# Values' products in the score buffers, a second bank for the MoE's first layer, and first keys and queries transposed by TensorE

## The chip, the core and the metric

The kernel runs on one core of one Trainium2 chip. The metric is the time of one execution on the device, in microseconds (us). TensorE (PE) does the matrix products, VectorE (DVE), ScalarE (ACT) and GpSimd (POOL) the elementwise work; SyncE (SP) and ACT start the transfers. Products land in PSUM, which has eight banks of 2 KB per partition; all else lies in SBUF.

## The reference

Block-sparse attention, then a two-layer network (here called the MoE) on its output:

```python
# q, k, v: (4, 8, 768, 64) float32; blocks of 32
scores = scale * np.matmul(q, k.transpose(0, 1, 3, 2))
# mask: neighbouring blocks, first and last block row and column, 3 sampled blocks per block row
scores = np.where(mask, scores, -1e9)
attn = softmax(scores)
x = np.matmul(attn, v)            # -> (3072, 512), heads side by side
h = x @ w_in                      # (512, 2048)
g = np.maximum(h, 0) + alpha * np.minimum(h, 0)
out = g @ w_out                   # (2048, 512)
```

w_in and w_out arrive as 64-bit floats.

## The kernel before

Every number of the products is held as two float16 halves, a high part and a rest ("hi" and "lo"), so that products of halves give nearly float32. Each tensor is scaled by a power of two for this.

The work is cut into 12 chunks: 4 batches, 3 chunks each, of 2 tiles of 128 rows (queries). A chunk has 4 units, one for each pair of heads; a unit has 4 steps (2 heads, 2 tiles), so there are 192 steps.

- A step (`attend`): PE makes the scores of 128 queries against 768 keys (`emit_s`, L498); both halves of keys are used through two layouts, `kt` and `ks`, the second with the halves of the partitions swapped. DVE adds the mask and takes the extreme of each row (`emit_bias`, L508). ACT does the exponential (`emit_exp`, L515) and the sum (L519), DVE the reciprocal (L523). The scaled P is split into hi (ACT L325 or DVE L327) and lo (POOL in two instructions, L335 and L336, in two of three steps, DVE L333 in the third), tile `ph`. A DMA transpose on the queue of SP gives `pt` (L538).
- A unit (`values`): PE multiplies transposed P by the values (`emit_av`, L552, 36 products), ACT and DVE split the result into the halves of `x` (L563, L568).
- A chunk of the MoE: 8 pieces of the first layer (`emit_up`, L852, 24 products each, tile `h`), the activation on DVE (L862, L863), the split on ACT (`gh`, L868) and POOL (`gl`, L873), and 8 pieces of the second layer (`emit_down`, L891, 12 products each, two tiles `o`). ACT scales and stores the output (L903).
- Preparation: keys of a batch are loaded (`kf`), squared and summed on ACT (L321), a product with ones gives the total over partitions (L421), DVE makes the scale, hi and lo are made (`kn`) and transposed by DMA (`kt`, L444), and two copies by DMA swap the halves (`ks`). Queries and values go the same way, the values without a transpose, the queries without a swap. w_in (`wi`) and w_out (`wo`) arrive as 64-bit numbers, and three instructions make float32 of each piece (`emit_n1` L708, `emit_n2` L713 or L715, `emit_n3` L720). A piece of w_in is a row of 128x512; a row of w_out comes in two halves of 128x256. The lo half of w_in is made by PE (L776, L777).

Nothing is ordered by hand. The program contains a planner (`Plan`): every operation is given to it with a due time (counted in steps), the engines that may do it with a cost in us on each, the operations it needs and the buffers that it takes and frees. The planner simulates the engines when the program is built and puts out one order, which is then the order of instructions of every engine. PSUM before: two score tiles `s` of two banks each, one bank `a` for the value products, one bank `h` for the first layer, two banks `o` for the second. Due times of the MoE lie `MOE_LAG` steps behind the end of a chunk's attention; those of w_in and w_out are `V_WI + W_WI * f` and `V_WO + W_WO * f` for row f of 16.

Of the kernel before, what the change touches and what calls it, by code (L numbers as in the profile page):

```python
# [54 lines left out]
class Plan:  # L55
# [5 lines left out]
    LAT = {"PE": 0.15, "DVE": 0.11, "ACT": 0.12, "POOL": 0.08}  # L61
# [4 lines left out]
    def buf(self, pool):  # L66
        return Buf(pool)
# [8 lines left out]
    def run(self):  # L76
# [16 lines left out]
        order = []  # L93
        busy = dict.fromkeys(self.ENGINES, 0.0)
# [78 lines left out]
def attn_moe(ctx: ExitStack, tc: tile.TileContext, q, k, v, sampled, w_in, w_out, alpha, out):  # L173
# [20 lines left out]
    plan = Plan(dict(bufs, s=2, a=1, h=1, o=2, ld=LD))  # L194
# [79 lines left out]
    bias = cpool.tile([P, NT, S], BF16, name="bias")  # L274
    nident = cpool.tile([P, P], F16, name="nident")
# [64 lines left out]
    MAX4 = {"DVE": (0.55, 1.1), "ACT": 0.85}  # L340
    LOW4 = {"DVE": (0.94, 1.5), "POOL": 2.8}
# [12 lines left out]
    kbuf, ksbuf, vbuf, qtbuf, ptbuf, xbuf = {}, {}, {}, {}, {}, {}  # L354
    o_s, o_kt, o_ks, o_v2, o_qt, o_cs, o_pt, o_x, o_sv = {}, {}, {}, {}, {}, {}, {}, {}, {}
# [91 lines left out]

    def emit_k_swap(e, b, hp):
# [92 lines left out]

    def emit_av(u):
# [4 lines left out]
        av = T["av", u] = ps_a.tile([P, W2], F32, tag="av", name="av")  # L547
# [25 lines left out]
    def prep_k(b, hp, prio, gate, pl):  # L573
# [4 lines left out]
        ab = plan.buf("o" if b == 0 else "a")  # L578
# [7 lines left out]
        o_kt[b, hp] = plan.op(prio - 2, {"SP": 2.4}, lambda: emit_k_t(b, hp), [o], [kbuf[b, hp]], [nb], dma=2.3)  # L586
        o_ks[b, hp] = plan.op(prio - 2, {"SP": 0.12}, lambda e: emit_k_swap(e, b, hp), [o_kt[b, hp]],
                              [ksbuf[b, hp]], [kbuf[b, hp]], dma=1.3)

    def prep_v(b, pl, prio, gate):  # L590
# [9 lines left out]
        ab = plan.buf("o" if b == 0 else "a")  # L600
# [8 lines left out]
    def prep_q(c, prio, pl, gate):  # L609
# [16 lines left out]
        for u, fb in zip(us, fbs):  # L626
            hp = units[u][1]
            p = prio if c == 0 else first[u] - 5
            nb = plan.buf("qn")
            o = plan.op(p, {"POOL": 0.35 + 0.25 * f, "ACT": 0.15 + 0.25 * f, "DVE": (0.1 + 0.15 * f, 0.2 + 0.4 * f)},  # L630
                        lambda e, u=u: emit_q_hi(e, u), [sc[hp]], [nb], [fb])
            o = plan.op(p, {"DVE": (0.14 + 0.27 * f, 0.2 + 0.65 * f)}, lambda u=u: emit_q_lo(u), [o], [], [nb, fb])
            qtbuf[u] = plan.buf("qt")
            o_qt[u] = plan.op(p - 2, {"SP": 0.8 * f}, lambda u=u: emit_q_t(u), [o], [qtbuf[u]], [nb], dma=0.75 * f)

    def attend(n):
# [5 lines left out]
        o_s[n] = o = plan.op(n, {"PE": 0.66}, lambda: emit_s(n), [o_qt[u], o_kt[b, hp], o_ks[b, hp]], [sb],  # L642
# [10 lines left out]
        o_pt[n] = plan.op(n - 1, {"SP": 2.4}, lambda: emit_p_t(n), [o],  # L653
                          [ptbuf[u, h]], [pb], dma=2.2)

    def values(u):
# [3 lines left out]
        ab = plan.buf("a")  # L660
# [3 lines left out]
        last = [o_pt[n] for n in range(first[u], first[u + 1])]  # L664
        o = plan.op(p - 2, {"PE": 0.4 + 1.92 * f}, lambda: emit_av(u), last + [o_v2[b, hp]],
# [18 lines left out]
    def emit_load_w(e, name, f, h):  # L684
# [112 lines left out]
    for f in range(NF):  # L797
        p = V_WI + W_WI * f
        o = plan.op(p - 12, LQ, lambda e, f=f: emit_load_w(e, "wi", f, 0), [n3wi[f - 8]] if f >= 8 else [], [plan.buf("ld")], dma=1.6)
        o = plan.op(p, {"DVE": (0.36, 0.6)}, lambda f=f: emit_n1("wi", f, 0), [o])  # L800
        o = plan.op(p, {"ACT": 1.27, "DVE": (0.6, 0.95)}, lambda e, f=f: emit_n2(e, "wi", f, 0), [o])
        n3wi[f] = plan.op(p, {"DVE": (0.61, 0.95)}, lambda f=f: emit_n3("wi", f, 0), [o])
        sqs[f] = plan.op(p, {"ACT": 0.65}, lambda f=f: emit_w_sq("wi", f), [n3wi[f]])
        if f % 2 == 1:
# [6 lines left out]
            for x in (f - 1, f):  # L811
                o = plan.op(p + 0.1, {"ACT": 0.63, "DVE": (0.36, 0.7), "POOL": 0.82}, lambda e, x=x: emit_w_hi(e, "wi", x), [gs[-1], prev])
# [4 lines left out]
                else:  # L817
                    prev = o_wi[x] = plan.op(p, {"DVE": (0.67, 1.1), "POOL": 2.3}, lambda e, x=x: emit_w_lo(e, "wi", x), [o], [], [sb])
    o_gsc = plan.op(V_WI + W_WI * NF - 2, {"DVE": 0.5}, emit_gsc, gs + [o_al])
    osq = []  # L820
    for f in range(NF):
# [3 lines left out]
        n3 = []  # L825
        for h in range(2):
            rb = plan.buf("vf" if h == 0 else "g")
            o = plan.op(p - 8 + 0.1 * h, LQ, lambda e, f=f, h=h: emit_load_w(e, "wo", f, h), [n3wi[min(NF - 1, 8 + f // 2)]], [rb, plan.buf("ld")], dma=0.8)
            o = plan.op(p, {"DVE": (0.22, 0.6)}, lambda f=f, h=h: emit_n1("wo", f, h), [o] + free, [], [rb])
            o = plan.op(p, {"ACT": 0.7, "DVE": (0.34, 0.5)}, lambda e, f=f, h=h: emit_n2(e, "wo", f, h), [o], [], [rb])  # L830
            n3.append(plan.op(p, {"DVE": (0.34, 0.5)}, lambda f=f, h=h: emit_n3("wo", f, h), [o], [], [rb]))
# [80 lines left out]
    def moe(c):  # L912
# [15 lines left out]
        for i, (kind, j) in enumerate(items):  # L928
            p = start + (stop - start) * i / len(items)
            if kind == "u":  # L930
# [79 lines left out]
```

## Time and profile before

| | |
|---|---|
| median of 3 runs | 908.3 us (907.07 to 909.03) |
| profiled execution | 911.63 us, of which the span from first to last instruction is 909.9 us |
| busy in the span | PE 802.7 us (88%), DVE 714.8 (79%), ACT 553.3 (61%), POOL 505.2 (56%) |
| granted clock of TensorE | 0.955 in the mean |
| DMA | 137.45 MB in 393236 packets |

An engine's busy time is a mean over stages that differ. The stretches shown below give it stage by stage: busy microseconds of each engine with the number of its instructions, then PE's granted clock, the DMA share and GB/s. A row of a group of instructions gives the line, the engine, the operation, out<-in, the shapes and the count, then busy time and mean nanoseconds of one, then the idle time before them and what ended it. A row of a wait gives who waited for whom, then microseconds in total, times and the longest. A row of the chain of work gives start, duration and what ran.

### The profile page before, as it was taken

The page shows a single profiled execution, that of the slowest core. Times are in us where ns is not written, and L with a number is a line of the kernel's source. Part 1 is how long each engine was busy: PE and PEld are TensorE (multiplying, and loading weights), DVE is VectorE, ACT ScalarE, POOL GpSimd, SP SyncE. Part 2 cuts the span into 40 slices and gives each one's busy share as a digit, 9 for nine tenths or more (in the row PEclk, how much of TensorE's full clock was granted, in tenths as well). Part 3 has the DMA queues.
Part 4 walks back from the last instruction along what each step waited for, and adds up shares of the span by engine and source line. Part 5 has one row for each costly group of instructions (what it writes and reads, how often), then busy time and mean ns, then how long its engine had stood idle before and what let it go on. Part 6 is the DMA issues. An engine that isn't in the chain of part 4 may idle for free.

```text
span 909.9 us, 16946 instructions
## 1 busy us (share of the span) xinstructions
PE 802.7 (88%) x6089; PEld 528.9 (58%) x6089; DVE 714.8 (79%) x1468; ACT 553.3 (61%) x1185; POOL 505.2 (56%) x413
## 2 busy tenths in 40 slices
PE   3757438988888999999989999999989999999998
PEld 1323215646555766666656766566656667666664
DVE  4899999997888898879987877688987887765232
ACT  6697667875755756757566565666566556664111
POOL 3154445775656667566576665456567566555221
PEclk9867767999999999999999999999999999999999
DMA  9997986988997876969976868969976868655000
GB/s 264 288 263 180 203 210 117 185 134 136 170 175 133 156 138 129 210 130 189 202 154 128 128 128 150 189 119 193 187 140 118 156 117 139 116 117 105 1 24 23
DMA packets 393236, 137.45 MB, mean 151 GB/s; under 512 B 355236, under 2 KB 383936, under 8 KB 393152
## 3 DMA queue, kind: packets, MB, share of 16 engines
q1 hardware_dynamic: 354816, 94.41, 60.2%
q10 hardware_dynamic: 38272, 41.95, 16.8%
q8 instruction: 47, 0.77, 0.3%
q14 instruction: 37, 0.30, 0.1%
q0 software_dynamic: 64, 0.02, 0.0%
HBM read 35.67 MB, written 6.29 MB: 46 GB/s over the span
## 4 chain that ended last, share of the span: by engine, by line
DVE 33%; PE 29%; issue 13%; ACT 12%; DMA 5%; POOL 4%; ACTq 2%; POOLq 0%; DVEq 0%
PE h L852 11%; PE o L891 10%; DVE e L508 6%; ACT e L515 5%; PE sp L498 4%; DVE g L862 4%; DVE ph L333 3%; PE av L552 3%; DVE ph L327 3%; ACT ph L325 2%; DVE g L863 2%; ACTq L364 2%; DMA kf<-in_k_dram 2%; DVE wo L720 2%; DVE qn L403 2%
## 5 line engine op out<-in xcount | busy, mean ns | idle before, releaser
L852 PE MATMUL h<-x,wi 128*128 128x256 f16 x2304 | 270.3, 274 | 14.9 <-DVE g L863 14.7
L852 PEld LDWEIGHTS <-wi 128*128 128x128 f16 x2304 | 227.1, 99 | 57.0 <-issue 18.4
L515 ACT ACTIVATE e<-e,nm 128x768 f32<-128x768 f32 x192 | 178.6, 930 | 114.4 <-DVE nm L508 106.7
L891 PE MATMUL o<-wo,gh 128*128 128x512 f16 x768 | 230.8, 382 | 0.0
L336 POOL TENSOR_TENSOR ph<-e,ph 128x768 f16<-128x768 f32 x128 | 216.7, 1693 | 10.7
L873 POOL TENSOR_TENSOR gl<-g,gh 128x512 f16<-128x512 f32 x96 | 119.1, 1241 | 177.8 <-ACT gh L868 173.4
L335 POOL TENSOR_SCALAR e<-e,rs 128x768 f32<-128x768 f32 x128 | 130.2, 1017 | 157.3 <-DVE ph L327 81.2
L508 DVE CUSTOM_DVE_ANT_0 e<-sp,bias,cs 128x768 f32<-128x768 f32 x192 | 191.9, 1008 | 17.0 <-PE sp L498 10.2
L891 PE MATMUL o<-wo,gl 128*128 128x512 f16 x384 | 146.4, 381 | 1.8 <-POOL gl L873 1.8
L868 ACT CAST gh<-g 128x512 f16<-128x512 f32 x96 | 59.1, 616 | 135.4 <-DVE g L863 120.1
L498 PE MATMUL sp<-kt,qt 128*128 128x512 f16 (+1 forms) x384 | 99.1, 341 | 46.7 <-DVE nm L508 46.5
L498 PEld LDWEIGHTS <-qt 128*128 128x128 f16 x768 | 74.4, 101 | 111.3 <-issue 58.4
L325 ACT ACTIVATE ph<-e,rs 128x768 f16<-128x768 f32 x114 | 105.8, 928 | 28.1 <-DVE rs L523 21.5
L891 PEld LDWEIGHTS <-gh 128*128 128x128 f16 x768 | 74.9, 99 | 80.0 <-issue 3.4
L862 DVE TENSOR_SCALAR g<-h,am 128x256 f32<-128x256 f32 x192 | 83.2, 474 | 48.3 <-PE h L852 46.7
L552 PE MATMUL av<-pt,v 128*64 128x256 f16 x1728 | 108.0, 281 | 1.8 <-DMA pt<-ph 1.5
L552 PEld LDWEIGHTS <-v 128*64 128x64 f16 x1728 | 93.6, 113 | 18.8 <-issue 14.7
L498 PE MATMUL sp<-ks,qt 128*128 128x512 f16 (+1 forms) x384 | 99.3, 342 | 0.0
L523 DVE RECIPROCAL rs<-dn 128x1 f32<-128x1 f32 x192 | 29.0, 156 | 76.0 <-ACT dn L519 75.1
L333 DVE SCALAR_TENSOR_TENSOR ph<-e,rs,ph 128x768 f16<-128x768 f32 x64 | 75.2, 1175 | 9.9 <-ACT ph L325 8.6
L863 DVE SCALAR_TENSOR_TENSOR g<-h,gsc,g 128x512 f32<-128x512 f32 x96 | 72.1, 751 | 3.4
L891 PEld LDWEIGHTS <-gl 128*128 128x128 f16 x384 | 37.8, 99 | 49.4 <-POOL gl L873 3.8
(119 smaller groups left out, 734.1 us busy)
## 6 DMA issues: line engine op xcount, KB each, us to landing
wo<-in_moe_w_in_dram ACTq DMA_DIRECT2D x16, 512.0 KB, 6.7
raw<-in_moe_w_out_dram ACTq DMA_DIRECT2D x32, 256.0 KB, 3.8
kf<-in_k_dram ACTq DMA_DIRECT2D x16, 384.0 KB, 4.1
qf<-in_q_dram ACTq DMA_DIRECT2D x48, 128.0 KB, 4.1
ks<-kt SPq DMA_DIRECT2D x32, 192.0 KB, 4.3
vf<-in_v_dram ACTq DMA_DIRECT2D x16, 384.0 KB, 7.6
out_dram<-ob ACTq DMA_DIRECT2D x24, 256.0 KB, 3.5
pt<-ph SPq DMA_TRANSPOSE x192, 4.1
```

Of the source, the lines that this page charges most:

```text
L325: nc.scalar.activation(dst, src, AF.Copy, scale=scale)
L333: nc.vector.scalar_tensor_tensor(dst, src, scale, hi, ALU.mult, ALU.subtract)
L335: nc.gpsimd.tensor_scalar(tmp, src, scale, 1.0, ALU.mult, ALU.mult)
L336: nc.gpsimd.tensor_tensor(dst, tmp, hi, ALU.subtract)
L498: nc.tensor.matmul(T["sp", n][:, a:z], T["qt", u][:, h, i, :], kt[:, h, a:z], start=(x == 0), stop=(x == 1))
L508: nc.vector.tensor_tensor_reduce(T["e", n], T["sp", n], bias[:, t0 + j % w, :], scale=T["cs", c][:, hp : hp + 1], scalar=3.0e38, op0=ALU.a ...
L515: nc.scalar.activation(T["e", n], T["e", n], AF.Exp, bias=T["nm", n], scale=-1.0, accum_out=T["su", n])
L552: nc.tensor.matmul(av[h * D : (h + 1) * D, : n * P], v2[:, h, t, vv, :], T["pt", u, h][:, pl * NT + t, :], start=(m == 0), stop=(m == len( ...
L852: nc.tensor.matmul(ph[:, i, :], win(w, f, ct), x[:, ct, :], start=(m == 0), stop=(m == len(terms) - 1))
L862: nc.vector.tensor_scalar(g[:, i, :], ph[:, i, :], 0.0, am1[:, f : f + 1], ALU.min, ALU.mult)
L873: nc.gpsimd.tensor_tensor(T["gl", c, j], T["g", c, j], T["gh", c, j], ALU.subtract)
L891: nc.tensor.matmul(T["o", c][t], g[:, i, t * P : (t + 1) * P], wout(w, f), start=(f == 0 and m == 0), stop=(f == NF - 1 and m == 2),)
```

## The change

- PSUM: the value products use the score tiles `s` (two tiles of two banks), the bank `a` is given up, and the first layer gets a second bank `h`. Totals of keys and values of later batches, which used bank `a`, use a bank `h`.
- Batch 0: keys and the swapped keys are transposed by PE into an `o` bank and copied to SBUF by ACT or DVE; the queries of chunk 0 also.
- Rows of w_out are loaded and unpacked whole (128x512), into the buffers of `x` or one of their own (`wr`), in place of halves in `vf` and `g`.
- POOL may make the hi half of P, keys and values.
- Buffers: `kt`, `ks`, `v2`, `vf` 5 to 4, `qf` 6 to 4, `ph` 4 to 5, `e` and `pt` 3 to 4; loads of weights in flight 4 to 5.
- The planner: other due times and costs, a model of DVE's and POOL's two-input or fast instructions holding each other up, and a score product is planned only after the value product of an older unit.

```diff
-MOE_LAG = 11.753
-MOE_BOOST = 7.325
-V_WI = -10.661
-W_WI = 1.102
-V_WO = 12.217
-W_WO = 1.038
+MOE_LAG = 9.585
+MOE_BOOST = 5.593
+V_WI = -1.832
+W_WI = 0.74
+V_WO = -2.974
+W_WO = 1.2
-PL_V = -12.594
-P_V = -6.546
+PL_V = -24.873
+P_V = 3.807
-LD = 4
+LD = 5
+P_PE = 0
+RAWP = ["x", "wr"]
+K_PE = 1
+Q_PE = 1
+BUFS = {"wr": 1, "vf": 4, "qf": 4, "qt": 3, "qn": 2, "ph": 5, "e": 4, "pt": 4, "x": 2, "g": 3, ...
...
-    LAT = {"PE": 0.15, "DVE": 0.11, "ACT": 0.12, "POOL": 0.08}
+    LAT = {"PE": 0.2, "DVE": 0.2, "ACT": 0.2, "POOL": 0.15}
+    SLACK = {"PE": 1.0, "DVE": 1.08, "ACT": 1.05, "POOL": 1.1, "SP": 1.0}
...
-            if isinstance(c, tuple):
-                c = c[1] if idle["POOL"] > now + 0.2 else c[0]
-            return c
+            return self.SLACK[e] * (sum(c) if isinstance(c, tuple) else c)
+
+        def hold(o, e):
+            c = o.alts[e]
+            if not isinstance(c, tuple):
+                return 0.0
+            if e == "DVE":
+                return max(port["to"] - now, 0.0) if port["from"] <= now else 0.0
+            return max(port["dve"] - now, 0.0) if c[0] == 0 else 0.0
...
-    ps_a = ctx.enter_context(tc.tile_pool(name="ps_a", bufs=1, space=PSUM))
-    ps_h = ctx.enter_context(tc.tile_pool(name="ps_h", bufs=1, space=PSUM))
+    ps_h = ctx.enter_context(tc.tile_pool(name="ps_h", bufs=2, space=PSUM))
...
-    MAX4 = {"DVE": (0.55, 1.1), "ACT": 0.85}
-    LOW4 = {"DVE": (0.94, 1.5), "POOL": 2.8}
+    MAX4 = {"DVE": (0.55, 0), "ACT": 0.85, "POOL": 1.05}
+    LOW4 = {"DVE": (0.94, 0), "POOL": (1.05, 1.65)}
...
+    def emit_k_pe(b, hp, x, h):
...
+        t = T["kp", b, hp, x, h] = ps_o.tile([P, 2 * DM], F16, tag="o", name="kp")
+        for i in range(NT):
+            g = h * NT + i
+            if x == 0:
+                nc.tensor.transpose(t[:, i * P : (i + 1) * P], nat[:, g].rearrange("p a d -> p (a d)"), ident16)
+                continue
+            for a in range(2):
+                nc.tensor.transpose(t[D * (1 - a) : D * (2 - a), i * P : (i + 1) * P], nat[:, g, a, :], ident16)
+
+    def emit_k_copy(e, b, hp, x, h):
+        key = ("kt", "ks")[x]
+        dst, src = T[key, b, hp][:, h].rearrange("p t j -> p (t j)"), T["kp", b, hp, x, h][:, :S]
+        if e == "ACT":
+            nc.scalar.copy(dst, src)
+        else:
+            nc.vector.tensor_copy(dst, src)
...
-        av = T["av", u] = ps_a.tile([P, W2], F32, tag="av", name="av")
+        av = T["av", u] = ps_s.tile([P, S], F32, tag="s", name="av")
...
-        o_s[n] = o = plan.op(n, {"PE": 0.66}, lambda: emit_s(n), [o_qt[u], o_kt[b, hp], o_ks[b, hp]], [sb],
+        o_s[n] = o = plan.op(n, {"PE": 0.66}, lambda: emit_s(n), [o_qt[u], o_av.get(steps[max(n - 3, 0)][0] - 2)] + o_kt[b, hp] + o_ks[b, hp], [sb],
...
-        if h == 0:
-            t = wt("vf", [P, 512], I32, "raw")
-        else:
-            t = wt("g", [P, 512], I32, "raw")
-        load(e, t, wo_src[:, f, h * 512 : (h + 1) * 512])
-        T["raw", name, f, h] = t
+        t = wt(h.pool, [P, 1024], I32, "raw")
+        load(e, t, wo_src[:, f, :])
+        T["raw", name, f, 0] = t
```

`emit_q_pe` and `emit_q_copy` do for queries what the two functions above do for keys: 4 transposes of 128x128 and one copy of 512 elements for each unit of chunk 0.

More of the change, by code (lines that the diff above doesn't have):

```diff
@@ L93, in run @@
         order = []
+        port = {"from": 0.0, "to": 0.0, "dve": 0.0}
         busy = dict.fromkeys(self.ENGINES, 0.0)
@@ L122, in run @@
                 for o in ready:
-                    if any(not b.live and self.free[b.pool] <= 0 for b in o.alloc):
+                    if any(not b.live and all(self.free[x] <= 0 for x in b.pools) for b in o.alloc):
                         continue
-                    best = min(o.alts, key=lambda e: max(idle[e] - now, 0.0) + load[e] + cost(o, e))
+                    best = min(o.alts, key=lambda e: max(idle[e] - now, hold(o, e)) + load[e] + cost(o, e))
+                    if hold(o, best) > 1e-9:
+                        continue
                     if idle[best] > now + 1e-9 or load[best] > 0:
@@ L129, in run @@
                     c = cost(o, best)
+                    if isinstance(o.alts[best], tuple):
+                        if best == "DVE":
+                            port["dve"] = now + c
+                        else:
+                            port["from"], port["to"] = now + self.SLACK[best] * o.alts[best][0], now + c
                     o.eng, o.start = best, now
@@ L133, in run @@
                     for b in o.alloc:
-                        self.free[b.pool] -= not b.live
+                        if not b.live:
+                            b.pool = next(x for x in b.pools if self.free[x] > 0)
+                            self.free[b.pool] -= 1
                         b.live = True
@@ L274, in attn_moe @@
     bias = cpool.tile([P, NT, S], BF16, name="bias")
+    ident16 = cpool.tile([P, P], F16, name="ident16")
+    nc.gpsimd.tensor_copy(ident16, ident)
     nident = cpool.tile([P, P], F16, name="nident")
@@ L418, in emit_k_norm @@
     def emit_k_norm(b, hp):
-        pool, tag = (ps_o, "o") if b == 0 else (ps_a, "av")
-        T["ktot", b, hp] = pool.tile([P, 512 if b == 0 else W2], F32, tag=tag, name="tot")
+        pool, tag = (ps_o, "o") if b == 0 else (ps_h, "h")
+        T["ktot", b, hp] = pool.tile([P, 512], F32, tag=tag, name="tot")
         nc.tensor.matmul(T["ktot", b, hp][:, 0:1], ones, T["kss", b, hp], start=True, stop=True)
@@ L446, in emit_k_t, with emit_q_pe, emit_q_copy @@
         )
+    def emit_k_pe(b, hp, x, h):
+        nat = T["kn", b, hp]
+        key = ("kt", "ks")[x]
+        if (key, b, hp) not in T:
+            T[key, b, hp] = wt(key, [P, 2, NT, P], F16)
+        t = T["kp", b, hp, x, h] = ps_o.tile([P, 2 * DM], F16, tag="o", name="kp")
[3 more added lines that the diff above has]
+                nc.tensor.transpose(t[:, i * P : (i + 1) * P], nat[:, g].rearrange("p a d -> p (a d)"), ident16)
+                continue
+            for a in range(2):
+                nc.tensor.transpose(t[D * (1 - a) : D * (2 - a), i * P : (i + 1) * P], nat[:, g, a, :], ident16)
+    def emit_k_copy(e, b, hp, x, h):
+        key = ("kt", "ks")[x]
+        dst, src = T[key, b, hp][:, h].rearrange("p t j -> p (t j)"), T["kp", b, hp, x, h][:, :S]
+        if e == "ACT":
+            nc.scalar.copy(dst, src)
+        else:
+            nc.vector.tensor_copy(dst, src)
+    def emit_q_pe(u):
+        n = chunks[units[u][0]][2]
+        T["qt", u] = wt("qt", [P, 2, n, P], F16)
+        T["qp", u] = ps_o.tile([P, 2 * DM], F16, tag="o", name="qp")
+        for g in range(2 * n):
+            nc.tensor.transpose(T["qp", u][:, g * P : (g + 1) * P], T["qn", u][:, g].rearrange("p a d -> p (a d)"), ident16)
+    def emit_q_copy(e, u):
+        n = chunks[units[u][0]][2]
+        dst, src = T["qt", u].rearrange("p h t j -> p (h t j)"), T["qp", u][:, : 2 * n * P]
+        if e == "ACT":
+            nc.scalar.copy(dst, src)
+        else:
+            nc.vector.tensor_copy(dst, src)
     def emit_k_swap(e, b, hp):
@@ L540, in emit_p_t, with emit_p_pe, emit_p_copy @@
         )
+    def emit_p_pe(n, x):
+        u, j = steps[n]
+        w = chunks[units[u][0]][2]
+        h, i = divmod(j, w)
+        if ("pt", u, h) not in T:
+            T["pt", u, h] = wt("pt", [P, 2 * NT, w * P], F16)
+        t = T["tp", n, x] = ps_o.tile([P, 2 * DM], F16, tag="o", name="tp")
+        for g in range(NT):
+            nc.tensor.transpose(t[:, g * P : (g + 1) * P], T["ph", n][:, x, g * P : (g + 1) * P], ident16)
+    def emit_p_copy(e, n, x):
+        u, j = steps[n]
+        w = chunks[units[u][0]][2]
+        h, i = divmod(j, w)
+        dst = T["pt", u, h][:, x * NT : (x + 1) * NT, i * P : (i + 1) * P]
+        src = T["tp", n, x][:, :S].rearrange("p (x j) -> p x j", j=P)
+        if e == "ACT":
+            nc.scalar.copy(dst, src)
+        else:
+            nc.vector.tensor_copy(dst, src)
     def emit_av(u):
@@ L585, in prep_k @@
         kbuf[b, hp], ksbuf[b, hp] = plan.buf("kt"), plan.buf("ks")
-        o_kt[b, hp] = plan.op(prio - 2, {"SP": 2.4}, lambda: emit_k_t(b, hp), [o], [kbuf[b, hp]], [nb], dma=2.3)
-        o_ks[b, hp] = plan.op(prio - 2, {"SP": 0.12}, lambda e: emit_k_swap(e, b, hp), [o_kt[b, hp]],
-                              [ksbuf[b, hp]], [kbuf[b, hp]], dma=1.3)
+        if b == 0 and K_PE:
+            for x, d, kb in ((0, o_kt, kbuf), (1, o_ks, ksbuf)):
+                d[b, hp] = []
+                for h in range(2):
+                    tb = plan.buf("o")
+                    t = plan.op(prio - 2, {"PE": 0.4 + 0.4 * x}, lambda x=x, h=h: emit_k_pe(b, hp, x, h), [o], [tb, kb[b, hp]], [nb])
+                    d[b, hp].append(plan.op(prio - 2, {"ACT": 0.85, "DVE": 0.9}, lambda e, x=x, h=h: emit_k_copy(e, b, hp, x, h), [t], [kb[b, hp]], [tb]))
+            return
+        o_kt[b, hp] = [plan.op(prio - 2, {"SP": 2.4}, lambda: emit_k_t(b, hp), [o], [kbuf[b, hp]], [nb], dma=2.3)]
+        o_ks[b, hp] = [plan.op(prio - 2, {"SP": 0.12}, lambda e: emit_k_swap(e, b, hp), o_kt[b, hp],
+                               [ksbuf[b, hp]], [kbuf[b, hp]], dma=1.3)]
     def prep_v(b, pl, prio, gate):
@@ L652, in attend @@
             ptbuf[u, h] = plan.buf("pt")
-        o_pt[n] = plan.op(n - 1, {"SP": 2.4}, lambda: emit_p_t(n), [o],
-                          [ptbuf[u, h]], [pb], dma=2.2)
+        if n < P_PE:
+            o_pt[n] = []
+            for x, src in ((0, o_hi), (1, o)):
+                tb = plan.buf("o")
+                t = plan.op(n - 2, {"PE": 0.4}, lambda x=x: emit_p_pe(n, x), [src], [tb, ptbuf[u, h]], [pb])
+                o_pt[n].append(plan.op(n - 2, {"ACT": 0.85, "DVE": 0.9}, lambda e, x=x: emit_p_copy(e, n, x), [t], [ptbuf[u, h]], [tb]))
+            return
+        o_pt[n] = [plan.op(n - 1, {"SP": 2.4}, lambda: emit_p_t(n), [o], [ptbuf[u, h]], [pb], dma=2.2)]
     def values(u):
@@ L663, in values @@
         p = first[u + 1] + 2
-        last = [o_pt[n] for n in range(first[u], first[u + 1])]
-        o = plan.op(p - 2, {"PE": 0.4 + 1.92 * f}, lambda: emit_av(u), last + [o_v2[b, hp]],
+        last = [x for n in range(first[u], first[u + 1]) for x in o_pt[n]]
+        o = o_av[u] = plan.op(p - 2, {"PE": 0.3 + 1.88 * f}, lambda: emit_av(u), last + [o_v2[b, hp]],
                     [ab, xbuf[c]], [ptbuf[u, 0], ptbuf[u, 1], vbuf[b, hp]])
@@ L811, in attn_moe @@
             for x in (f - 1, f):
-                o = plan.op(p + 0.1, {"ACT": 0.63, "DVE": (0.36, 0.7), "POOL": 0.82}, lambda e, x=x: emit_w_hi(e, "wi", x), [gs[-1], prev])
+                o = plan.op(p + 0.1, {"ACT": 0.63, "DVE": (0.36, 0), "POOL": 0.82}, lambda e, x=x: emit_w_hi(e, "wi", x), [gs[-1], prev])
                 if WI_LO == "pe":
@@ L817, in attn_moe @@
                 else:
[L818 removed]
+                    prev = o_wi[x] = plan.op(p, {"DVE": (0.67, 0), "POOL": (0.8, 1.25)}, lambda e, x=x: emit_w_lo(e, "wi", x), [o], [], [sb])
     o_gsc = plan.op(V_WI + W_WI * NF - 2, {"DVE": 0.5}, emit_gsc, gs + [o_al])
@@ L824, in attn_moe @@
         free = [n3wi[s]] if s < NF else []
[L825 to L831, printed above, removed]
+        rb = plan.buf(*RAWP)
+        o = plan.op(p - 8, LQ, lambda e, f=f, rb=rb: emit_load_w(e, "wo", f, rb), [n3wi[min(NF - 1, 8 + f // 2)]], [rb, plan.buf("ld")], dma=1.6)
+        o = plan.op(p, {"DVE": (0.36, 0)}, lambda f=f: emit_n1("wo", f, 0), [o] + free, [], [rb])
+        o = plan.op(p, {"ACT": 1.27, "DVE": (0.6, 0)}, lambda e, f=f: emit_n2(e, "wo", f, 0), [o], [], [rb])
+        n3 = [plan.op(p, {"DVE": (0.61, 0)}, lambda f=f: emit_n3("wo", f, 0), [o], [], [rb])]
         osq.append(plan.op(p, {"ACT": 0.65}, lambda f=f: emit_w_sq("wo", f), n3))
@@ L839, in attn_moe @@
     for f in range(NF):
-        o = plan.op(p + 0.1 * f, {"ACT": 0.63, "DVE": (0.36, 0.7), "POOL": 0.82}, lambda e, f=f: emit_w_hi(e, "wo", f), [o_swo, prev])
-        prev = o_wo[f] = plan.op(p + 0.1 * f, {"DVE": (0.67, 1.1), "POOL": 2.3}, lambda e, f=f: emit_w_lo(e, "wo", f), [o])
+        o = plan.op(p + 0.1 * f, {"ACT": 0.63, "DVE": (0.36, 0), "POOL": 0.82}, lambda e, f=f: emit_w_hi(e, "wo", f), [o_swo, prev])
+        prev = o_wo[f] = plan.op(p + 0.1 * f, {"DVE": (0.67, 0), "POOL": (0.8, 1.25)}, lambda e, f=f: emit_w_lo(e, "wo", f), [o])
     def emit_up(c, j):
```

47 lines of the change are left out of this document (27 added, 20 removed).

## The prediction

> **What bounds the kernel now.** I read first the table of stretches, to see which engine is full in which stage, then what TensorE (PE) waits for in each, then the groups of VectorE (DVE) in the stage where time is lost.
>
> ```profile
> core 0: us, PE busy (x) PEld busy (x) DVE busy (x) ACT busy (x) POOL busy (x), PEclk, DMA share, GB/s
> 0.00:45.00 45.00, 24.46 (x70) 12.39 (x71) 29.57 (x88) 29.62 (x65) 11.43 (x28) 0.92 1.04 274
> 45.00:182.00 137.00, 88.87 (x555) 52.88 (x554) 130.57 (x285) 105.34 (x235) 74.27 (x59) 0.76 0.87 193
> 182.00:300.00 118.00, 102.97 (x796) 66.33 (x794) 100.20 (x192) 73.34 (x156) 74.32 (x59) 0.97 0.87 152
> 300.00:750.00 450.00, 430.88 (x3472) 291.84 (x3470) 373.94 (x748) 282.50 (x612) 279.38 (x216) 1.00 0.83 152
> 750.00:870.00 120.00, 119.98 (x972) 82.94 (x971) 70.24 (x145) 56.84 (x110) 57.71 (x47) 1.00 0.51 96
> 870.00:909.90 39.90, 35.50 (x235) 22.55 (x232) 10.27 (x19) 5.66 (x9) 8.08 (x7) 1.00 0.04 14
> ```
>
> PE is idle for 909.9 - 802.7 = 107.2 us in all: 20.5 before 45 us, 48.1 up to 182, 15.0 up to 300, 19.1 up to 750, 4.4 at the end. Between 45 and 182 us DVE is busy for 130.6 of 137: that stage waits on DVE. From 300 us on PE is 96% busy and later full, so whatever starts MoE work earlier is kept to the end: PE runs out of idle time, not of work. The forecast is therefore a sum over PE's 107 us. The waits name them, for 0 to 182, 182 to 300 and 300 to 750 us in turn:
>
> ```profile
> PE sp L498 <- DVE nm L508: 34.3, 13, 7.4
> PE h L852 <- DVE g L863: 1.2, 2, 0.9
> ...
> PE sp L498 <- DVE nm L508: 10.5, 9, 3.5
> PE h L852 <- DVE g L863: 2.5, 1, 2.5
> ...
> PE h L852 <- DVE g L863: 11.0, 10, 2.1
> PE sp L498 <- DVE nm L508: 1.7, 3, 1.0
> ```
>
> Early on, a score product waits until DVE has read an older score tile out of its buffer (46.5 us in all). Later the commonest wait is the first MoE layer's: its one bank must be read by the activation (14.7 us in all).
>
> **The change part by part.** (1) *w_out is unpacked in whole rows.* 32 half rows of 256 become 16 rows of 512. What DVE paid (45 to 182 us), and what w_in's rows, which have the new shape already, cost over the whole run:
>
> ```profile
> L720 DVE SCALAR_TENSOR_TENSOR wo<-raw,wo 128x256 int32<-128x256 int32 x32 | 23.4, 751 | 1.5 <-ACT raw L713 1.3
> L708 DVE TENSOR_SCALAR wo<-raw 128x256 int32<-128x256 int32 x32 | 11.1, 377 | 0.0
> L715 DVE SCALAR_TENSOR_TENSOR wo<-raw,wo 128x256 int32<-128x256 int32 x17 | 8.0, 486 | 0.0
> ...
> L720 DVE SCALAR_TENSOR_TENSOR wi<-wo,wi 128x512 int32<-128x512 int32 x16 | 12.5, 786 | 0.2 <-ACT wo L713 0.2
> L715 DVE SCALAR_TENSOR_TENSOR wi<-wo,wi 128x512 int32<-128x512 int32 x13 | 8.8, 679 | 0.1
> L708 DVE TENSOR_SCALAR wi<-wo 128x512 int32<-128x512 int32 x16 | 6.6, 423 | 0.0
> ```
>
> Before: 23.4 + 11.1 + 8.0 = 42.5 us. After, by the means of w_in: 16 x (0.786 + 0.423) + 8.5 x 0.679 = 25.1, so 17.4 less. That is the upper end, since the half rows' means hold stalls:
>
> ```profile
> L708 DVE TENSOR_SCALAR wo<-raw x32: 269/280/1726, 74.0 to 142.1; 128x256 int32<-128x256 int32 x32
> L720 DVE SCALAR_TENSOR_TENSOR wo<-raw,wo x32: 396/414/1871, 75.6 to 147.9; 128x256 int32<-128x256 int32 x32
> ...
> L336 POOL TENSOR_TENSOR ph<-e,ph 128x768 f16<-128x768 f32 x20 | 35.3, 1767 | 1.7
> ```
>
> By the medians 32 x (0.280 + 0.414) + 8.0 = 30.2, so 12.3 of the 42.5 us are stalls, of up to 1.5 us each, about as long as one of GpSimd's (POOL's) 1.77 us subtractions in the same stretch. Without stalls the gain is 30.2 - (16 x (0.423 + 0.68) + 5.8) = 6.7, with 0.68 the time of the undisturbed w_in rows (0.679 above). I take 9, near the low end: the POOL subtractions stay, and a saturated DVE has always some instruction in front of them. The Trainium skill, "SBUF — State Buffer", section "SBUF: two separate sides", gives that reason: DVE and GpSimd share a port pair under an exclusive lock, and the loser blocks for the whole instruction. The trace's maxima agree with it, and by that rule alone the stalls follow the number of POOL instructions, not of DVE's, and this part is worth 6.7 us.
>
> The rows now lie in the x buffers and one of their own, three in place of eight halves; if DVE catches up with the loads it waits there.
>
> (2) *First keys and queries go through TensorE.* Out of the queue of SP go 4 transposes of keys, 8 half swaps and 4 transposes of queries. In the first 45 us queue q1 carries nothing but these (four of the half swaps and one transpose of queries come later):
>
> ```profile
> q1 hardware_dynamic: 8224, 2.75, 32.8%
> ...
> L508 DVE CUSTOM_DVE_ANT_0 e<-sp,bias,cs x17: 1003/1005/1018, 44.0 to 117.6; 128x768 f32<-128x768 f32 x17
> ...
> DVE e L508 <- PE sp L498: 3.1, 1, 3.1
> ...
> L308 ACT ACTIVATE bias<-mkr 128x768 bf16<-128x768 f32 x6 | 4.6, 805 | 1.1 <-PE mkr L293 1.1
> L781 ACT CAST wi<-d 128x512 f16<-128x512 f32 x16 | 9.4, 587 | 4.0 <-PE d L777 4.0
> ```
>
> They took 0.328 x 45 = 14.8 us of all DMA engines there, which are full there (share 1.04). The first score's pass on DVE starts at 44.0 us; it could start near 20. But DVE waits for scores only 3.1 us in these 45, the rest of its 15.4 idle us being mostly the wait for first loads. Added: 144 + 16 transposes on PE, at 0.11 each (24 products of 256 columns take 2.62 us, a row below) 17.5 us in a stage where PE idles 20.5, on no path; and 16 copies of 768 at about 0.8 (the bias copy) plus 4 of 512 at 0.59, 15.2 us. ACT has 15.4 idle us there and DVE as many; were all to fall on DVE later, they would cost up to 12. I take 3 gained, from -12 to +5. POOL, SP: nothing is added, SP loses its queue head.
>
> (3) *Order of weights and MoE.* The due time of the first MoE layer moves from 11.753 to 9.585 steps behind its chunk: 2.17 steps. One step costs DVE in the DVE-bound stage 30.9 (bias pass) + 12.2 + 8.8 (the P split) + 4.3 (reciprocal) over 31 steps = 1.8 us:
>
> ```profile
> L508 DVE CUSTOM_DVE_ANT_0 e<-sp,bias,cs 128x768 f32<-128x768 f32 x31 | 30.9, 1006 | 3.5 <-PE sp L498 3.5
> ...
> L333 DVE SCALAR_TENSOR_TENSOR ph<-e,rs,ph 128x768 f16<-128x768 f32 x10 | 12.2, 1224 | 0.1
> ...
> L327 DVE TENSOR_SCALAR ph<-e,rs 128x768 f16<-128x768 f32 x10 | 8.8, 884 | 0.0
> ...
> L523 DVE RECIPROCAL rs<-dn 128x1 f32<-128x1 f32 x30 | 4.3, 152 | 2.8 <-ACT dn L519 2.6
> ```
>
> So PE is fed 2.17 x 1.8 = 4 us sooner (0, if the weights come later, to 137/31 x 2.17 = 9.6, if a step's whole pace counts). I take 4. w_in's due times come later, w_out's earlier; the work is the same, 0.
>
> (4) *POOL may take the first half of P, K and V.* Each P taken saves DVE 0.88 us and costs POOL about 1.1 (the row below, of this stretch); POOL's 62.7 idle us there cover it. The stalls just named may grow by as much. 0, from -4 to +4.
>
> ```profile
> L335 POOL TENSOR_SCALAR e<-e,rs 128x768 f32<-128x768 f32 x20 | 22.9, 1144 | 45.9 <-ACT ph L325 18.1 <-DVE ph L327 16.4 <-DMA pt<-ph 7.9
> ```
>
> (5) *Second bank for the first layer.* The 14.7 us of waits should go. What is late next is the same activation on DVE or POOL's remainder, so of the 13.5 us after 182 I take 9 (0 to 14.7). Sums of squares of later batches now pass through one of these two banks, 15 times; inside the 9.
>
> (6) *Values' product takes a score buffer.* It occupies one of two, 48 times, for its product and two reads:
>
> ```profile
> 502.09 2.09 PE av L552 x36
> ...
> 504.93 2.62 PE h L852 x24
> 507.55 0.65 PE sp L498 x4
> ...
> L852 PE MATMUL h<-x,wi x2304: 269/273/421, 146.8 to 899.7; 128*128 128x256 f16 x192
> L563 ACT ACTIVATE x<-av x48: 357/364/384, 93.4 to 845.2; 128x256 f16<-128x256 f32 x48
> L568 DVE SCALAR_TENSOR_TENSOR x<-av,x x48: 404/414/426, 93.8 to 845.6; 128x256 f16<-128x256 f32 x48
> ```
>
> 2.09 + 0.364 + 0.414 = 2.9 us at least. Four scores of a unit hold a buffer for 1.7 us each at least (0.65 product, 1.0 DVE), so 9.5 of 2 x 19 us per unit are needed (909.9 / 48): room, but queued behind a score that waits is all of PE's later work, and DVE's passes wait for that score. Lower bound 0, upper 48 x 0.78 (PE waiting through both reads) = 37. I take a loss of 3, because PE usually holds MoE products to put in between.
>
> (7) *Buffers and gates.* Keys, values, raw keys and raw queries lose one or two, e, P and transposed P gain one. Loads for the next batch stand in the chain of waits:
>
> ```profile
> 215.75 9.33 DMA kf<-in_k_dram
> ...
> 627.17 7.46 DMA kf<-in_k_dram
> ```
>
> A longer or shorter wait at each of three changes of batch: 0, from -10 to +6. The other new planner costs and the wait for an older value product act only on the order, 0; if that order fits DVE's real stalls better, the gain is in the second rival.
>
> The sum, against the profiled execution's 911.63 us (909.9 of span and 1.7 around it): -9 - 3 - 4 + 0 - 9 + 3 + 0 = -22, 889.6. The median of the runs, 908.3, is 3.3 lower, so **886**. The forecast's own range, with the small terms moved, is 875 to 896.
>
> **The rivals.** *The shared score buffer becomes the wait (slower).* If PE stands still for more than 25/48 = 0.52 us at each value product, the gains of 25 are gone; at the full 0.78 it is 908.3 - 25 + 37 = 920. For it: the wait of scores on DVE is PE's largest already. Against it: after 300 us it is under 2 us in all, as PE has MoE work between.
>
> *The start lets go altogether.* 17.4 for the rows, 5 for the keys, 9.6 for the order, 4 on POOL, 14.7 in the first layer, less 3: 47.7, so about 861. For it: 48 idle PE us in the DVE-bound stage are there to be had. Against it: stalls must vanish that POOL still causes.
>
> *The start does not move.* Rows without stalls 6.7, nothing from keys and order, 5 from the bank, less 3: 8.7, so 900. For it: the DMA share before 182 us is 0.87 to 1.04, so loads may be late next, with three raw buffers in place of eight. Against it: 14.8 us of DMA work go from there.
>
> *No effect*, gains and losses even: 908.
>
> **How the numbers follow.** 0.45 for the forecast, 0.15 for the large gain, 0.17 for the start that stays, 0.05 for no effect, 0.18 for the slower one. A difference under 0.2% is about what a measurement cannot tell from none. Faster is 0.45 + 0.15 + 0.17 = 0.77, same 0.05, slower 0.18. The range from 862 to 911 leaves out about half of the large gain and two thirds of the slower case, 0.19.
>
> **What would show it.** Right: the wait of h on g under 4 us; PE's waits for scores before 182 us under 22 in place of 34.3; first MoE product some 15 us before the 146.8 us of the row above; rows of w_out at 128x512 with about 25 to 36 us in all on DVE; no q1 packets in the first 20 us. Wrong: scores waiting on the reads of av, or PE idle after 300 us over 20; DVE waiting for raw rows; DVE's instructions longer than before.

## The result and the profile after

The changed kernel takes 878.6 us (median of 4 runs, 876.5 to 881.2) against 907.7 us of the kernel before on the same chip: a ratio of 0.968, 95% interval 0.965 to 0.972. That is 29 us less; 22 were forecast, and the time lies in the range. Ratios here and below leave out the one slow execution, 1666.4 us, among the ten of the PSUM part alone. The profiled execution took 879.08 us, 877.1 of them span. The table of stretches of the changed kernel, as above, PE first:

```profile
0.00:45.00 45.00, 26.66 (x212) 17.14 (x213) 30.01 (x81) 29.55 (x62) 16.13 (x32) 0.92 0.81 236
45.00:182.00 137.00, 91.73 (x537) 52.52 (x536) 129.82 (x246) 98.13 (x224) 92.74 (x68) 0.79 0.79 175
182.00:300.00 118.00, 114.68 (x911) 75.69 (x908) 104.62 (x209) 82.94 (x179) 84.82 (x66) 1.00 0.87 163
300.00:750.00 450.00, 447.13 (x3663) 306.46 (x3662) 368.17 (x763) 291.56 (x634) 305.54 (x241) 1.00 0.87 158
750.00:850.00 100.00, 100.00 (x792) 68.65 (x791) 52.83 (x106) 40.06 (x78) 46.27 (x38) 1.00 0.44 81
850.00:877.10 27.10, 22.69 (x147) 13.90 (x144) 6.51 (x12) 3.81 (x6) 4.69 (x5) 1.00 0.05 20
```

PE is busy for as long as before (802.9 us, 802.7 then), and idle for 74.2 us where it was 107.2. The place of the 33 us is the surprise: 2.2 before 45 us, 2.9 up to 182, 11.7 up to 300, 16.2 up to 750. The stage that waits on DVE hardly let go; everything behind it did. DVE's passes over the scores and the first MoE products, after the change:

```profile
L569 DVE CUSTOM_DVE_ANT_0 e<-sp,bias,cs x31: 994/1005/1018, 25.7 to 178.6; 128x768 f32<-128x768 f32 x31
...
L948 PE MATMUL h<-x,wi x2304: 269/273/417, 148.8 to 866.9; 128*128 128x256 f16 x192
```

The first pass came 18 us sooner (25.7 for 44.0), yet by 182 us 31 passes had been made in both kernels, and the first MoE product came at 148.8 us, not before 146.8. Over the whole run PE's waits are now:

```profile
PE sp L559 <- DVE nm L569: 23.7, 9, 5.2
PE tot L445 <- ACT junk L344: 8.4, 4, 5.7
PE sp L559 <- DVE x L650: 6.0, 6, 3.1
...
PE av L634 <- DVE nm L569: 1.7, 1, 1.7
```

The wait of h on g is gone altogether (14.7 before), that of scores on DVE's passes is halved (46.5 before), and the new one, of scores and value products on one another's buffer, is 6.0 + 1.7 us. A product for the mask, which lies in the score tiles too, waits 4.7 us for a pass.

### The profile page after: what moved, and what is told of

It reads as the page before. It is cut to its first block, busy times and chain, and to the rows that moved or that the text cites. A ratio compares the mean times of both kernels' runs of the same rounds, so it can differ in the third digit from the quotient of the medians.

```text
span 877.1 us, 17172 instructions
## 1 busy us (share of the span) xinstructions
PE 802.9 (92%) x6249; PEld 534.4 (61%) x6249; DVE 692.0 (79%) x1413; ACT 546.0 (62%) x1178; POOL 550.2 (63%) x446
## 4 chain that ended last, share of the span: by engine, by line
PE 64%; DVE 18%; issue 6%; ACT 3%; DMA 2%; POOL 1%; ACTq 1%; POOLq 0%; DVEq 0%
PE o L987 22%; PE h L948 22%; PE sp L559 11%; PE av L634 9%; DVE e L569 4%; DVE ph L356 2%; DMA kf<-in_k_dram 2%; DVE wo L818 1%; DVE wo L813 1%; ACT e L576 1%; DVE v L356 1%; DVE g L958 1%; DVE wo L356 1%; DVE wo L806 1%; ACT ph L348 1%
## 5 line engine op out<-in xcount | busy, mean ns | idle before, releaser
L359 POOL TENSOR_TENSOR ph<-e,ph 128x768 f16<-128x768 f32 x128 | 223.0, 1742 | 10.7
L358 POOL TENSOR_SCALAR e<-e,rs 128x768 f32<-128x768 f32 x128 | 134.3, 1049 | 113.9 <-ACT ph L348 63.1
L348 ACT ACTIVATE ph<-e,rs 128x768 f16<-128x768 f32 x106 | 97.7, 928 | 15.7 <-DVE rs L584 15.3
L634 PE MATMUL av<-pt,v 128*64 128x256 f16 x1728 | 104.8, 276 | 1.7 <-DVE nm L569 1.7
L634 PEld LDWEIGHTS <-v 128*64 128x64 f16 x1728 | 91.6, 111 | 22.1 <-issue 17.0
L356 DVE SCALAR_TENSOR_TENSOR ph<-e,rs,ph 128x768 f16<-128x768 f32 x64 | 82.6, 1291 | 4.9 <-ACT ph L348 4.7
L352 POOL TENSOR_SCALAR ph<-e,rs 128x768 f16<-128x768 f32 x35 | 35.3, 1008 | 50.7 <-DVE rs L584 37.6
```

Source lines behind the costliest of these rows:

```text
L348: nc.scalar.activation(dst, src, AF.Copy, scale=scale)
L356: nc.vector.scalar_tensor_tensor(dst, src, scale, hi, ALU.mult, ALU.subtract)
L358: nc.gpsimd.tensor_scalar(tmp, src, scale, 1.0, ALU.mult, ALU.mult)
L359: nc.gpsimd.tensor_tensor(dst, tmp, hi, ALU.subtract)
L634: nc.tensor.matmul(av[h * D : (h + 1) * D, : n * P], v2[:, h, t, vv, :], T["pt", u, h][:, pl * NT + t, :], start=(m == 0), stop=(m == len( ...
```

## The experiments

**One bank, same order.** Only the physical number of banks is changed; every engine's order of instructions is that of the changed kernel.

```diff
-    ps_h = ctx.enter_context(tc.tile_pool(name="ps_h", bufs=2, space=PSUM))
+    ps_h = ctx.enter_context(tc.tile_pool(name="ps_h", bufs=1, space=PSUM))
```

> The changed kernel with its order of instructions kept on every engine, but the first layer's tile h has one PSUM bank in place of two (the other stays empty). Theory A, the second bank took away the waits after 182 us: PE again waits for h on g, 15 us or more in all (the kernel before: 14.7), and the time is 893 to 910. Theory B, the new order did it and would do with one bank: the wait stays under 5 us in all and the time is 879 to 884.

912.3 us (ratio to the kernel before 1.006, 1.002 to 1.010), 34 us over the changed kernel. Its longest waits of PE:

```profile
PE sp L559 <- DVE nm L569: 21.8, 8, 5.4
PE h L948 <- DVE g L959: 12.7, 13, 3.0
PE h L948 <- DVE mm L535: 10.5, 3, 5.2
PE tot L445 <- DVE g L959: 7.5, 4, 1.9
```

The order of the changed kernel cannot do without the second bank: 30.7 us of waits stand on it, about as many as the gain. Of them 12.7 are the wait of h on g, a little under the 15 that Theory A named; the other 18.0 are waits around the totals (`tot`, `mm`), which now share the one bank with `h`. Theory A's mechanism holds for this order, and the time is somewhat above its range. What one bank would cost in an order made for it is the next question.

**The old PSUM, planned anew.** The value products get their own bank back, the first layer one bank.

```diff
-    ps_h = ... bufs=2
-        av = T["av", u] = ps_s.tile([P, S], F32, tag="s", name="av")
+    ps_a = ... bufs=1
+    ps_h = ... bufs=1
+        av = T["av", u] = ps_a.tile([P, W2], F32, tag="av", name="av")
```

> The changed kernel with the PSUM of before: value products in a bank of their own, one bank h, no planner's wait for older value products; the planner makes a new order for it. Theory A (the PSUM part carries the gain after 182 us): 895 to 905. Theory B (order, costs and buffers carry it): 878 to 886, and waits for h under 5 us.

889.2 us (0.980, 0.974 to 0.986), between the two theories: 10.6 us over the changed kernel, 18 under the one before. The wait of h on g is back with 10.8 us. So the PSUM part is worth about a third of the gain beside the other changes, and the rest stays without it.

**The PSUM part alone, in the kernel before.** The same lines the other way round, with the old planner, buffers and due times.

> The kernel before with the PSUM part alone (value products in the score tiles, two banks h, the planner's wait for older value products), all costs, due times and buffers as before; the planner makes a new order. Theory A: 888 to 896, with the wait of h on g under 3 us. Theory B: 904 to 912.

906.8 us (1.000, 0.996 to 1.003): nothing. The waits tell why:

```profile
PE sp L498 <- DVE nm L508: 30.7, 18, 5.4
PE av L552 <- DVE nm L508: 22.6, 14, 4.4
PE sp L498 <- DVE x L568: 9.1, 10, 1.8
```

The second bank's gain was there (2.0 us of waits of h on g, from 14.7), but the value products now wait 22.6 us for a score tile that DVE has yet to read, and scores 9.1 us for the reads of the value products. That is the prediction's first rival, the shared buffer as the new wait, and in this order it eats what the bank gives.

**Shallow buffers.** 3 tiles e, 4 ph and 3 pt, as before.

```diff
-"ph": 5, "e": 4, "pt": 4
+"ph": 4, "e": 3, "pt": 3
```

> The changed kernel with 3 tiles e, 4 ph and 3 pt, as before, in place of 4, 5 and 4. Theory F, the deeper buffers let scores run ahead and so keep the shared score tiles from blocking PE: 890 to 905, with waits of value products or scores on DVE of over 10 us after 182 us. Rival: the depth matters little, 877 to 883.

954.1 us (1.054, 1.050 to 1.057): 76 us slower than the changed kernel, far beyond what Theory F asked for. Its waits of PE, DVE's passes with what they waited for, and the stretch from 300 to 750 us:

```profile
PE av L634 <- DVE nm L569: 32.1, 12, 3.7
PE sp L559 <- DVE nm L569: 24.4, 15, 4.5
PE d L874 <- POOL sid L869: 16.6, 4, 5.5
...
L569 DVE CUSTOM_DVE_ANT_0 e<-sp,bias,cs 128x768 f32<-128x768 f32 x192 | 192.0, 1009 | 30.0 <-PE sp L559 15.2 <-POOL ph L359 10.3 <-POOL e L358 2.2
...
300.00:750.00 450.00, 410.56 (x3172) 279.58 (x3170) 323.89 (x673) 268.20 (x578) 266.55 (x213) 0.94 0.76 142
```

PE idles 39 us between 300 and 750 us in place of 2.9, and DVE is less busy too (324 us for 368): no engine is short, each waits for another. With three e a new bias pass must wait until POOL has done the lo half of three steps back, and the passes waited 12.5 us for POOL. The score tile stays full meanwhile, and with it the one that the value product needs. How these waits grow to 39 us of PE through the order that was planned for them is argued, not shown by a run.

**The new buffers alone, in the kernel before, and with the PSUM part.**

```diff
-    bufs = dict(kt=5, ks=5, v2=5, vf=5, qf=6, qt=3, qn=2, ph=4, e=3, pt=3, ...
+    bufs = dict(kt=4, ks=4, v2=4, vf=4, qf=4, qt=3, qn=2, ph=5, e=4, pt=4, ...
```

> The kernel before with the buffer counts of after alone (e, ph, pt one more; kt, ks, v2, vf one and qf two fewer), planned anew by its old planner. Theory F, depth itself carries the gain: 880 to 895. Rival G, depth is worth what the order makes of it, and the old costs and due times make little of it: 898 to 915.

> The kernel before with the PSUM part and the buffer counts of after, old planner and due times. Theory F: the waits of the value products for a score tile (22.6 us with the PSUM part alone) fall under 8 us and the time is 878 to 892. Rival G: they stay above 12 us, 898 to 912.

914.5 us (1.007, 1.004 to 1.010) and 918.8 us (1.012, 1.009 to 1.016). Theory F falls for the kernel before: depth by itself gains nothing there. With both, the value products' wait for a score tile all but went (3.6 us, from 22.6), as F said, but the time did not follow: PE's waits for scores grew to 38.4 us before 182 us and 18.6 us after 300 (24.4 and 10.1 with the PSUM part alone). Rival G is the nearer in time, once at the end of its range and once over it, but the waits that it named were not the ones.

**The planner's model.** Latencies of before, no margins, and no holding of DVE against POOL. This is not the model of before, which priced DVE's hi half at 1.1 us in place of 0.55 while POOL was busy; here it is 0.55 always.

```diff
-    LAT = {"PE": 0.2, "DVE": 0.2, "ACT": 0.2, "POOL": 0.15}
-    SLACK = {"PE": 1.0, "DVE": 1.08, "ACT": 1.05, "POOL": 1.1, "SP": 1.0}
+    LAT = {"PE": 0.15, "DVE": 0.11, "ACT": 0.12, "POOL": 0.08}
+    SLACK = {"PE": 1.0, "DVE": 1.0, "ACT": 1.0, "POOL": 1.0, "SP": 1.0}
...
-            if not isinstance(c, tuple):
+            if True:
                 return 0.0
```

> The changed kernel whose planner has the latencies of before, no margins on costs, and no holding of DVE against POOL. Theory E, the planner's truer model gives an order that fits the real stalls: 888 to 905, with PE idle over 10 us between 300 and 750 us. Rival, the model matters little beside buffers and due times: 876 to 884.

939.6 us (1.038, 1.034 to 1.040), 61 us slower, beyond Theory E's range in its direction, with PE idle for 29 us between 300 and 750 us. The model decides which engine takes an operation; the hi half of P here (first fence), in the changed kernel (second) and what DVE took of it in the kernel before (third):

```profile
L350 DVE TENSOR_SCALAR ph<-e,rs 128x768 f16<-128x768 f32 x105 | 100.2, 955 | 2.4
...
L348 ACT ACTIVATE ph<-e,rs 128x768 f16<-128x768 f32 x60 | 55.7, 932 | 20.0 <-DVE rs L584 18.2 <-DVE kn L356 1.4
...
L352 POOL TENSOR_SCALAR ph<-e,rs 128x768 f16<-128x768 f32 x27 | 30.8, 1140 | 44.6 <-DVE rs L584 40.0 <-PE tot L445 2.6 <-PE sp L559 2.0
```

```profile
L348 ACT ACTIVATE ph<-e,rs 128x768 f16<-128x768 f32 x106 | 97.7, 928 | 15.7 <-DVE rs L584 15.3
...
L350 DVE TENSOR_SCALAR ph<-e,rs 128x768 f16<-128x768 f32 x51 | 44.7, 883 | 0.7
...
L352 POOL TENSOR_SCALAR ph<-e,rs 128x768 f16<-128x768 f32 x35 | 35.3, 1008 | 50.7 <-DVE rs L584 37.6 <-PE kp L481 8.0 <-PE o L987 5.1
```

```profile
L327 DVE TENSOR_SCALAR ph<-e,rs 128x768 f16<-128x768 f32 x78 | 64.3, 827 | 1.1
```

Believing that DVE does it in 0.55 us, this model gives it 105 of 192; there they take 0.955 in the mean, and DVE is busy for 765 us in all, where the changed kernel has 692. ACT, which takes 0.93 in both, stands at 503 us for 546. Latencies, margins and holding were taken out together; what each is worth is not shown.

**Due times of before.** The eight numbers go back. The planner's test for free buffers is changed besides, so that it counts all that an operation takes at once; with the changed kernel's own numbers that test gives the same order, so what differs comes from the numbers.

```diff
-MOE_LAG = 9.585
+MOE_LAG = 11.753
...
-V_WO = -2.974
+V_WO = 12.217
```

> The changed kernel with the eight due-time numbers of before (MOE_LAG, MOE_BOOST, V_WI, W_WI, V_WO, W_WO, PL_V, P_V), planned anew. Theory C, the due times let PE off its waits: 890 to 905, the waits of value products or scores on DVE's reads come back after 182 us (over 10 us). Theory D, the planner's costs or the buffers do it: 877 to 884. By the prediction's term (3) it would be 4 us slower (0 to 9.6).

895.0 us (0.989, 0.986 to 0.992): 16 us slower, and the waits on score tiles after 182 us are 15.4 us (1.7 in the changed kernel): Theory C, in time and in the waits that it named.

**No hi halves on POOL.**

```diff
-    MAX4 = {"DVE": (0.55, 0), "ACT": 0.85, "POOL": 1.05}
+    MAX4 = {"DVE": (0.55, 0), "ACT": 0.85}
```

> The changed kernel without POOL's share in the hi halves of P, keys and values (35 + 8 instructions on POOL go to ACT and DVE). Prediction's term (4): 0, from -4 to +4, so 875 to 883. Rival, that relief of DVE is what the gain lived on: 885 to 895, with more waits of PE on DVE's passes.

870.3 us (0.961, 0.957 to 0.964): faster than both kernels, by 8 us than the changed one. Where (the changed kernel's row is in the table above):

```profile
45.00:182.00 137.00, 100.41 (x591) 58.97 (x592) 128.43 (x265) 111.19 (x244) 82.55 (x63) 0.78 0.81 185
```

PE gains 8.7 busy us in the stage that waits on DVE, ACT takes 13 more, POOL 10 less, and 33 passes are made by 182 us in place of 31. DVE's instructions are shorter: the hi half of P takes 0.828 us in the mean for 0.883, the lo half 1.214 for 1.291. In this pair of plans the option in term (4) was a loss, not a zero.

**Half rows, same order.** Each unpacking instruction on a row of w_out becomes two on halves of 256.

```diff
-        nc.vector.tensor_scalar(d, r, 3, 0x3FFFFFFF, ALU.logical_shift_left, ALU.bitwise_and)
+        for a, z in halves(name):
+            nc.vector.tensor_scalar(d[:, a:z], r[:, a:z], 3, 0x3FFFFFFF, ALU.logical_shift_left, ALU.bitwise_and)
```

> The changed kernel with its order kept, but each unpacking instruction on a row of w_out is two on halves of 256, as before. Prediction's term (1): DVE pays 6.7 to 17.4 us more on these rows before 182 us, and as that stage waits on DVE, the time grows by 7 to 17 us (886 to 896). Rival: the start's gain is lost anyway (both kernels had made 31 score passes by 182 us), so the time grows by under 3 us.

885.3 us (0.976, 0.970 to 0.982): 6.7 us more, just under the expected 7 to 17. The rival's 3 us are unlikely, not excluded: the executions of the two kernels do not overlap (876.5 to 881.2 and 882.4 to 887.4), but the intervals of their ratios do by a little. DVE's rows with halves and, in the second fence, of the changed kernel:

```profile
L820 DVE SCALAR_TENSOR_TENSOR wo<-raw,wo 128x256 int32<-128x256 int32 x28 | 17.7, 674 | 0.0
...
L826 DVE SCALAR_TENSOR_TENSOR wo<-raw,wo 128x256 int32<-128x256 int32 x32 | 16.4, 555 | 0.0
...
L810 DVE TENSOR_SCALAR wo<-raw 128x256 int32<-128x256 int32 x32 | 8.8, 318 | 3.2 <-DMA raw<-in_moe_w_out_dram 3.2
```

```profile
L818 DVE SCALAR_TENSOR_TENSOR wo<-raw,wo 128x512 int32<-128x512 int32 x16 | 14.0, 878 | 0.2 <-ACT raw L811 0.2
...
L813 DVE SCALAR_TENSOR_TENSOR wo<-raw,wo 128x512 int32<-128x512 int32 x14 | 11.6, 831 | 0.0
...
L806 DVE TENSOR_SCALAR wo<-raw 128x512 int32<-128x512 int32 x16 | 9.9, 625 | 1.7 <-DMA raw<-in_moe_w_out_dram 1.7
...
L806 DVE TENSOR_SCALAR wo<-raw x16: 406/418/1860, 72.9 to 148.6; 128x512 int32<-128x512 int32 x16
L818 DVE SCALAR_TENSOR_TENSOR wo<-raw,wo x16: 672/682/2016, 76.9 to 151.8; 128x512 int32<-128x512 int32 x16
L813 DVE SCALAR_TENSOR_TENSOR wo<-raw,wo x14: 675/684/1308, 73.9 to 142.4; 128x512 int32<-128x512 int32 x14
```

42.9 us against 35.5. By the medians whole rows would take 16 x (0.418 + 0.682) + 14 x 0.684 = 27.2, so 8.3 us are stalls; halves with their medians of 0.281, 0.413 and 0.416 would take 33.9, so 9.0 are. In the same order, twice as many instructions meet about the same stalls. The Trainium skill, "SBUF — State Buffer", section "SBUF: two separate sides", describes a lock on a port pair that DVE and GpSimd share, held for a whole instruction; the two totals agree with that, as far as they go.

**First keys and queries by DMA.** Planned anew.

```diff
-K_PE = 1
-Q_PE = 1
+K_PE = 0
+Q_PE = 0
```

> The changed kernel with keys of batch 0 and queries of chunk 0 transposed by DMA again, planned anew. Prediction's term (2): 3 us slower (from 5 faster to 12 slower), 879 to 884. Rival, the early start of the scores is what the steady stage lives on: over 890; or it is given back by the DVE-bound stage: 876 to 880, with the first score pass back near 40 us.

889.1 us (0.980, 0.976 to 0.984): 10.5 us slower, three times the term, above the 879 to 884 expected and just under the rival's 890. The first score comes at 57.7 us and the first MoE product at 164.5, and PE is busy for 101.1 us before 182 where the changed kernel has 118.4 (12.6 of that difference are the transposes themselves). By 182 us 28 passes have been made in place of 31. But the largest wait of PE in this order is another one, that of scores on the reads of value products, with 17.3 us in three waits; so what of the 10.5 us is the later start alone is not shown.

**A repeat.** Meant as a change without weight.

```diff
-MOE_LAG = 9.585
+MOE_LAG = 9.385
```

> The changed kernel with MOE_LAG 9.385 in place of 9.585: a fifth of a step, which by term (3) is worth 0.4 us. It measures what the planner makes of a change that means nothing: if the time stays within 876 to 881, differences over 4 us between planned kernels carry a cause of their own; if it moves by 8 us or more, single planned kernels do not tell causes of that size apart.

879.0 us (0.968, 0.964 to 0.972). The order came out the same instruction for instruction, so this run only repeats the kernel, in another session than its first 878.6. The kernel before had medians of 905.1 to 908.2 in its sessions, so differences of more than about 4 us between the medians given here are not drift of the measurement. How far a meaningless new plan moves the time stays open, and with it the causes of single planned kernels that lie a few us apart.

## Why the prediction was right, and where its sum was not

The sign and the time came out, the sum by terms that failed in opposite ways; that 886 lies so near to 878.6 is in part luck. What was said of PE, that it runs out of idle time and not of work, held: 33 us of span less, 33 us of idle time less. By its steps:

- (1) Whole rows: 9 us taken, near the low end of 6.7 to 17.4. With the order kept, the half rows cost 6.7 us of time, and DVE 6.7 us of undisturbed work: right, and for the reason given. Between the two kernels DVE paid 7.0 less (42.5 to 35.5), mostly for another reason. ACT took only 2 of 16 rows where half were assumed, so the undisturbed work fell by 2.0 only (29.2 to 27.2, all three rows by their medians; the prediction left the third, L715, at its mean), and the stalls fell from 13.3 to 8.3.
- (2) Keys and queries: 3 us taken, 10.5 by the undoing, twice the 5 that the term allowed as a gain; its bound of 12 lay on the side of a loss, and the expectation before the undoing has the two the wrong way round. The transposes took 12.6 us of PE, not 17.5. Against the kernel before, the early start brought no more passes by 182 us.
- (3) Due times: 4 us taken, 16 by the undoing, above the upper bound of 9.6. The term priced a step on DVE; that w_in's and w_out's rows moved among the steps was put at 0.
- (4) POOL: 0 taken, a loss of 8, outside the bound of 4.
- (5) and (6) Second bank 9, shared buffer -3, so 6 together; 10.6 by the undoing, but 0 alone in the kernel before. The rival that ended slower named the right wait; in the old order it cost the whole gain, in the new one 7.7 us.
- (7) Buffers and planner costs, put at 0 (from -10 to +6): here the prediction failed most. Taking back the depth costs 76 us and taking out the model 61, both far outside. Neither is a gain of that size over the kernel before, since the other numbers were kept as they stand beside it: the new buffers in the old kernel made it 0.7% slower. The smaller numbers of key, value and query buffers were not undone by themselves.

So the 16 us forecast for the start were 5, and the 6 us forecast behind it 28. What is shown with the order kept: the second bank carries 34 us of this order and the whole rows 6.7. Undone with a new plan, PSUM part, due times, first keys, model and depth each cost 10 to 76 us, and PSUM part and depth gain nothing in the kernel before; that these two pay only beside the others is shown by that, how much of each number is the luck of a plan is not.

The simulation that each program runs when it is built, without the chip, shows where these costs arise. It ends at 853.9 us for the changed kernel, and at 863.7, 872.4, 875.1 and 944.9 us with PSUM part, first keys, due times and depth undone: 9.8, 18.5, 21 and 91 us later, where the chip took 10.6, 10.5, 16 and 76 us more. So these losses stand in the planned orders already, though not each in its size. Without margins, holding and the new latencies it ends at 851.1 us and the chip takes 939.6: that plan looks as good, but the engines do not keep to its times.

Not tried is the new model alone in the kernel before; it would say whether the model is what lets the others pay.

Of the signs named, h on g under 4 us, w_out's rows between 25 and 36 us, PE idle under 20 us after 300 (7.3) and no q1 traffic in the first 20 us came true. The first MoE product 15 us sooner did not, and PE's waits for scores before 182 us, 28.0 with the new kind, did not fall under 22. Of the signs of being wrong, PE idle after 300 us stayed away, and three came in part: scores wait for the reads of av (6.0 us), DVE waits for raw rows (1.7 us), and DVE's instructions are longer (lo half of P 1.291 us in the mean for 1.175, hi half 0.883 for 0.827).

## What to carry to other kernels

Where a planner sets the order, check its assumed durations, and what it leaves out, against the trace before anything else: without latencies, margins and holding, and with an operation entered at 0.55 us that takes 0.955, the order lost 61 us. A buffer that two products share pays only if each engine that reads it comes in time, so look for the wait on it, not for its load. And an option for a second engine may slow the first: take it away and look.

## What was not expected of the hardware

In one order, the stalls of DVE on w_out's rows did not grow with the number of its instructions (8.3 and 9.0 us for 46 and 92 of them). Across orders the number of POOL's subtractions does not give them either: 13.3 us in the kernel before, 8.3 in the changed one and 3.6 without POOL's hi halves, with 13, 12 and 13 subtractions between 70 and 155 us. What sets them beyond that is not shown.

The granted clock of PE fell even late in a run where PE idled most. Between 300 and 750 us it was 0.94 with shallow buffers (39.4 us idle), 0.99 without the planner's model (29.4), and 1.00 in the kernel before (19.1) and the changed one (2.9). The two do not go strictly together: with one bank in the kept order it was 0.99 at 16.0 us.
